# Moving tail products, a projection piece and an input scaling between the segments of a recurrent forward stage

## The chip, the core and the metric

The kernel runs on one core of one Trainium2 chip. A core has five engines with queues of their own: TensorE (PE in the profile; its weight loads are PEld), VectorE (DVE), ScalarE (ACT), GpSimd (POOL) and SyncE (SP, which here only issues DMAs). The metric is the device time of one launch in microseconds; it was 2993.81, the median of three runs (2991.97 to 2997.16).

## The reference

The program computes a forward pass and all its gradients (`jax.vjp`). Only the forward part of the attention is touched by the change. Its core, cut from the reference, with 2048 rows of width 512, 32 heads of 128, segments of 32 rows and a memory of 8 rows:

```python
mem = mem0
for s in range(n_seg):                       # 64 segments, one after the other
    xs = x[:, s * seg_len:(s + 1) * seg_len, :]
    h = jnp.concatenate([mem, xs], axis=1)   # 8 + 32 rows
    q, k, v = (einsum('btd,dhe->bhte', h, W) for W in (Wq, Wk, Wv))
    scores = einsum('bhqe,bhke->bhqk', q, k) * scale
    p = softmax(where(mask, scores, -1e9))
    o = einsum('bhqk,bhke->bhqe', p, v)
    o = einsum('bhte,hed->btd', o, Wo)
    mem = o[:, :M, :]                        # the next segment's memory
    outs.append(o[:, M:, :])
```

Ahead of it stands the modulation: `mod = silu(c) @ w_mod`, six rows of 512, two of which scale and shift the layer norm of `x` (the input to the segments), and four of which are needed only behind the attention. The memory rows of a segment's output are the first rows of the next segment's input, so the 64 segments form a recurrence.

## The kernel before

The forward stage is `phase2`: one Python loop over the segments (`for s in range(NS)`), with `s4 = s % 4`, the segment's place in its tile of four (128 input rows). Every engine's instructions run in the order in which the loop writes them: `self.pin(i0)` at its end ties each instruction to the one before it on the same engine. Work that doesn't belong to a segment's own chain is written into chosen places of the loop.

A segment's own chain, in its order on TensorE: projection of K and Q (`proj`, L673 and L257 by helper, 32 products each, in four column groups of 32), V chunk 0, the turn of K and Q (`turns`, L851), V chunk 1, the scores (`st_exp`, L861, exponentials on ScalarE at L863), V chunk 2, the row sums (`den`, L867) and the products with V (`pv`, L887), the scaling by the row sums into `Ost` (`ost`: L911 on VectorE, L908 on ScalarE), its transposes into `OT` (`ott_first`, `ott_rest`, L879 and L921), the out-projection (`outproj`, 64 products, L223), the split of its result into a rounded half `at_hi` (ScalarE, L230) and the rest `at_lo` (VectorE, L232), the fold that sums the four row groups (`sum_pair`, `at_ft`, L242), and the copy of the eight memory rows into the next segment's `hT` (L1065). That copy is where this document draws the border between segments.

A segment of 40 rows is 8 memory rows and 32 input rows, and the four column groups of TensorE hold 32 rows each. So 8 rows of each segment, its tail, are left over, and the tails of the four segments of a tile are done together:

- The tail rows of K and Q of tile t + 1 (`b_pieces`, from the input rows in `hb`, into RBk and RBq) are projected in tile t: K in two pieces of four steps, Q in pieces of two, four and two. The dictionary that `b_pieces` gives says in which segment and at which place a piece runs: `"turn"` is ahead of `ott_first`, `"f1"` is between the out-projection and the fold, `"f2"` is behind the copy into `hT`. `fill(s4, where)` runs what is entered in `slots`.
- The tail rows of V ride in the free fourth column group of the V chunks (`VTAILS`).
- The tail rows of the attention output are collected in `ao_tail` through a tile (`tail.collect`, POOL). Their 32 out-projection products come in pieces of 8, 16 and 8 (`TailRows`, `tail.chunk()`), into one PSUM tile `ao_tps`. When the third is done, `tail.split()` rounds it into `ao_b_hi` (ScalarE) and `ao_b_lo` (VectorE) and puts the fold on the list `later`; `pop_later` takes it from there in a following segment (`ao_b_ft`, eight small products), and one segment behind that come its transpose and four stores.

Also in the loop: the input tile's norm in five steps, `p1(j, k)`: k = 0 loads, 1 takes the statistics (VectorE, then a power on POOL), 2 scales (two VectorE instructions, L411 and L412), 3 shifts (L416, and a store), 4 turns the tile (four transposes on TensorE, then copies into `hx` and `hb`). Tile j is three tiles ahead in steps 0 to 2 and two in steps 3 and 4. And the sixteen pieces of the late modulation rows (`mod_rest`): one segment issues the load of 128 columns of `w_mod` on SP, the next one runs eight products at place f2, then a copy on ScalarE and a store on POOL. `mod_at` lists the segments of the products.

PSUM: all of this shares one ring of five buffers (tag "p"), the scores have three of their own. ScalarE also writes the mask into the score buffers (`mask_copy`). The places, in the order of the loop from the scores on:

```python
st_exp(0..2); v_chunk(s, 2); v_tails(s + 1)
if s4 == 3: tail.chunk()                # place A: eight tail products
den, pv, ost ...; fill(s4, "turn"); ott_first(); ott_rest(); outproj()
p1 ...; tails_in("kq", s + 1)           # ahead of the split
parts = self.split_pair(sb2, at_ps, "at")
fill(s4, "f1")
if s4 == 3: tail.chunk()                # sixteen
ft = self.sum_pair(...); copy into hT; masks; fill(s4, "f2"); modulation
if s4 == 3: tail.chunk()                # eight
tail.split(); self.store_rows(...)
```

Of the kernel before, what the change touches and what calls it, by code (L numbers as in the profile page):

```python
# [40 lines left out]
class K:  # L41
# [403 lines left out]
    def phase2(self):  # L445
# [15 lines left out]
        with ExitStack() as ctx:  # L461
# [43 lines left out]
            def p1(j, k=None, defer=None):  # L505
                if j < NT:
                    if j not in p1s:
                        p1s[j] = p1_tile(j)
                    for i in (range(1, 5) if k is None else [k]):
                        r = p1s[j][i]()  # L510
                        if r is not None:
                            if defer is None:
                                hxs[j] = r()
                            else:
                                defer.append(lambda: hxs.update({j: r()}))
# [102 lines left out]
            def b_pieces(t):  # L618

                bt = btails[t] = {}  # L620
                RBt = RB

                def proj_b(x, a, n, eng):
                    hb = hxs[t][1]
                    self.col_pass(psp, Ws[x], 0, lambda c: hb[:, c, :, :].rearrange("p s q -> p (s q)"), RBt[x], eng, steps=(a, n))
                    if a + n == 8:
                        store = lambda: rows_out(RBt[x], DR[x], t * nseg_t, nseg_t)
                        if t == 0:
                            first_stores.append(store)
                        else:  # L630
                            store()

                def turn_b(x):
                    bt[x] = btp.tile([128, 8, 128], BF16, name="b_cols" + x)
                    tp = psp.tile([128, 8, 128], BF16, name="turn_ps", tag="p")
                    for i in range(8):
                        nc.tensor.transpose(tp[:, i, :], RBt[x][:, i * 128:(i + 1) * 128], self.ident[:, :])

                    def f():
                        for hf in range(2):  # L640
                            self.evac(("act", "dve")[hf], bt[x][:, 4 * hf:4 * hf + 4, :], tp[:, 4 * hf:4 * hf + 4, :])

                    evacs.append(f)

                P = lambda x, a, n, eng: (lambda: proj_b(x, a, n, eng))
                T_ = lambda x: (lambda: turn_b(x))
                if t == 0:
                    return {"k": [P("k", 0, 4, "dve"), P("k", 4, 4, "dve"), T_("k")], "q": [P("q", 0, 4, "dve"), P("q", 4, 4, "dve"), T_("q")]}
                return {(0, "f1"): [P("k", 0, 4, "dve")], (1, "f1"): [P("k", 4, 4, "dve")], (1, "f2"): [P("q", 0, 2, "act")],
                        (2, "turn"): [T_("k")], (2, "f1"): [P("q", 2, 4, "dve")], (2, "f2"): [P("q", 6, 2, "act")],  # L650
                        (3, "turn"): [T_("q")]}

# [126 lines left out]
            first_tile = first_tile_steps()  # L779
            norms = []  # L780
            mod_r = []
            mod_at = sorted([4 * i + 4 for i in range(4 * DC - 1)] + [7])
            def rows_b(rb, b):

                for i in range(4):
# [38 lines left out]
            for s in range(NS):  # L824
                s4 = s % nseg_t
                if s4 == 2:
                    p1(s // nseg_t + P1_AHEAD + 1, 0)
                if s4 == 0:
                    slots = b_pieces(s // nseg_t + 1) if s + nseg_t < NS else {}
                hT = get_ht(s)  # L830
                hT_next = get_ht(s + 1) if s + 1 < NS else None
                QT, KT, Vst = XT["q"], XT["k"], Vsts[s % 2]
# [81 lines left out]
                def ott_first():  # L914
                    ps, n = transposes_part(Ost, 0, m=120)
                    self.evac("dve", part3(OT, 0)[:, 0:n, 0:120], ps)
# [82 lines left out]
                    v_tails(s + 1)  # L999
                if s < NS - 1:  # L1000
                    nc.sync.dma_start(VTr[:], Vst[:, :], transpose=True)
                if s4 == 3:
                    tail.chunk()
                or2 = ps_f32("or_ps")
                den(0, or2)
                den(1, or2)
# [8 lines left out]
                ost(0, or0, "dve")  # L1015
                ost(1, or1, "act")
                den(2, or2)
                early = s4 == 0 and len(self.later) > 1
                pv(2, or2)
                recip(2, 3, or2)  # L1020
                ost(2, or2, "dve")
                fill(s4, "turn")
                if s == 3 or s4 == 1 and s > 1:
                    p1(s // nseg_t + P1_AHEAD, 4, evacs)
                if s == NS - 1:
                    turn_v(2)
                ott_first()
                if early:
                    self.pop_later()
# [8 lines left out]
                nc.sync.dma_start(self.OSR[s], gl3(Ost))  # L1038
                at_ps = outproj()
                evac_turned()  # L1040
                if s < 3:
                    p1(P1_AHEAD, s + 1)
                if s4 != 1 and s > 0:
                    p1(s // nseg_t + P1_AHEAD + (s4 > 0), {2: 1, 3: 2, 0: 3}[s4])
                if NS - 4 <= s < NS - 1:
                    first_tile[s - NS + 4]()
                elif s == NS - 1:
# [1 line left out]
                if s + 1 < NS:  # L1049
                    tails_in("kq", s + 1)  # L1050
                parts = self.split_pair(sb2, at_ps, "at")
                tail.collect(s4, [OT])
                nc.sync.dma_start(self.OT[s], gl3(OT))
                fill(s4, "f1")
                if s == NS - 1:
                    first_tile[7]()
                    nc.scalar.activation(self.first_st[:, 11:12], self.first_st[:, 10:11], AF.Sigmoid)
                if s4 == 3:
                    tail.chunk()
                if s == NS - 1:  # L1060
                    turn_p(0)
# [9 lines left out]
                if s + 1 in mod_at:  # L1071
                    load, products = self.mod_rest(psp, sb2, mod_at.index(s + 1))
                    load()
                    mod_r.append(products)
                if s4 == 3:
                    tail.chunk()
                tail.split()
                self.store_rows(psp, sb2, ft, self.AOA[s + 1, 0:32, :], "at", "p")
# [1372 lines left out]
```

## Time and profile before

| | |
|---|---|
| median of three runs | 2993.81 us |
| the profiled execution | 2993.29 us, span 2991.5 us |
| forward loop | to about 970 us |
| segments 0, 1, 2, 3 of most tiles | 13.96, 13.96, 14.39, 15.23 us |
| TensorE's granted clock over the span | 0.996 |

The span runs from the first to the last instruction; 1.8 us of the profiled execution's time lie around it. In group lines the columns are line, engine, operation, written and read tiles, shapes and count. In the table of stretches each row is a stretch, its length, the busy time (and count) of PE, PEld, DVE, ACT and POOL, the granted clock, DMA share and GB/s. In the timeline each row is a start, a length, the engine and its instruction, and in brackets the idle time before it and what ended it. A product's length in the timeline contains some 0.2 to 0.4 us of passage through the array, so work on TensorE is read from start to start. A number "into" a segment counts from the copy into `hT` that starts it.

### The profile page before, as it was taken

The page shows a single profiled execution, that of the slowest core. Times are in us where ns is not written, and L with a number is a line of the kernel's source. Part 1 is how long each engine was busy: PE and PEld are TensorE (multiplying, and loading weights), DVE is VectorE, ACT ScalarE, POOL GpSimd, SP SyncE. Part 2 cuts the span into 40 slices and gives each one's busy share as a digit, 9 for nine tenths or more (in the row PEclk, how much of TensorE's full clock was granted, in tenths as well). Part 3 has the DMA queues.
Part 4 walks back from the last instruction along what each step waited for, and adds up shares of the span by engine and source line. Part 5 has one row for each costly group of instructions (what it writes and reads, how often), then busy time and mean ns, then how long its engine had stood idle before and what let it go on. Part 6 is the DMA issues. An engine that isn't in the chain of part 4 may idle for free.

```text
span 2991.5 us, 105396 instructions
## 1 busy us (share of the span) xinstructions
PE 2916.3 (97%) x43816; PEld 1819.9 (61%) x43816; DVE 1625.0 (54%) x3680; ACT 1347.8 (45%) x3244; POOL 1237.0 (41%) x2485
## 2 busy tenths in 40 slices
PE   6999999999999999999999999999999999999999
PEld 3666666666666544446577777777777754445455
DVE  5566556566555788833455566666556632850011
ACT  3666666666666533312355555555555520110011
POOL 2455555545555222221244444444444422762111
PEclk8999999999999999999999999999999999999999
DMA  9988888888889899998699999999999997786565
GB/s 308 223 224 212 213 211 221 212 216 213 213 214 274 211 231 232 230 277 285 202 248 243 250 251 240 258 256 252 249 252 254 245 280 247 251 263 193 158 217 172
DMA packets 837922, 703.01 MB, mean 235 GB/s; under 512 B 537682, under 2 KB 709890, under 8 KB 836548
## 3 DMA queue, kind: packets, MB, share of 16 engines
q1 hardware_dynamic: 711828, 485.29, 66.5%
q0 software_dynamic: 54512, 148.63, 15.8%
q10 hardware_dynamic: 71104, 62.34, 6.5%
q8 instruction: 345, 5.65, 0.8%
q14 instruction: 133, 1.09, 0.1%
HBM read 294.99 MB, written 276.35 MB: 191 GB/s over the span
## 4 chain that ended last, share of the span: by engine, by line
PE 65%; DMA 2%; DVE 1%; ACT 1%; issue 1%; POOL 0%; DVEq 0%; SPq 0%; POOLq 0%; ACTq 0%
PE gps L2232 14%; PE dh_ps L215 8%; PE g_ps L1855 5%; PE pass_ps L257 5%; PE gps5o L2247 4%; PE dhq_ps L223 4%; PE mm L1336 3%; PE dh_tps L215 3%; PE gps L1515 3%; PE mm L1296 2%; PE mm L1311 2%; PE tps L1772 2%; PE mm L1269 1%; PE mm L1265 1%; PE gps L1414 1%; PE dp_ps L1832 1%
## 5 line engine op out<-in xcount | busy, mean ns | idle before, releaser
L2232 PE MATMUL gps<-rows,hrows 128*128 128x512 bf16 (+2 forms) x2160 | 415.5, 356 | 0.0
L2232 PEld LDWEIGHTS <-hrows 128*128 128x128 bf16 x2160 | 211.2, 98 | 204.5 <-issue 0.9
L63 DVE CAST ot<-gps 128x512 bf16<-128x512 f32 (+3 forms) x76 | 48.2, 634 | 309.0 <-PE gps L2232 229.0
L1083 POOL TENSOR_TENSOR Pst<-Pst,rden 120x1408 bf16<-120x1408 bf16 x63 | 159.8, 2536 | 96.0 <-issue 54.3
L1900 POOL COPY dOst<-RAd 96x512 bf16<-96x512 bf16 x128 | 75.2, 611 | 300.5 <-DVE RAd L63 299.6
L61 ACT ACTIVATE ot<-gps 128x512 bf16<-128x512 f32 (+3 forms) x75 | 41.2, 549 | 350.5 <-PE gps L2232 215.1
L673 PE MATMUL pass_ps<-Wv,hT 128*32 128x512 bf16 (+2 forms) x2304 | 186.7, 357 | 0.0
L2236 POOL DMA_DIRECT2D out_dram<-ot x104 | 78.5, 755 | 256.0 <-DVE ot L63 132.9
L257 PEld LDWEIGHTS <-hT 128*32 128x32 bf16 x4096 | 115.3, 97 | 98.0 <-POOL hT L559 4.7
L63 DVE CAST Vst<-pass_ps 96x512 bf16<-96x512 f32 x128 | 87.1, 681 | 106.7 <-ACT RBv L61 98.1
L215 PE MATMUL dh_ps<-WvT,dVT 128*32 128x512 bf16 x2048 | 133.9, 381 | 1.8 <-DVE RBd L63 0.2
L223 PE MATMUL at_ps<-Wo,OT 128*32 128x256 bf16 x4096 | 128.8, 276 | 1.8 <-ACT OT L61 1.0
L673 PE MATMUL pass_ps<-Wv,hb 128*32 128x512 bf16 (+2 forms) x636 | 127.5, 349 | 2.2 <-DMA Wv<-in_A_Wv_dram 2.2
L257 PE MATMUL pass_ps<-Wk,hT 128*32 128x512 bf16 x2048 | 123.5, 382 | 2.5 <-DVE mv L402 1.1
L257 PE MATMUL pass_ps<-WoT,dyT 128*32 128x256 bf16 (+1 forms) x3072 | 123.3, 308 | 1.5 <-ACT dyT L1981 0.9
L223 PE MATMUL dhq_ps<-WqT,dQT 128*32 128x256 bf16 x4096 | 123.1, 273 | 0.4 <-issue 0.4
L257 PE MATMUL pass_ps<-Wq,hT 128*32 128x512 bf16 x2048 | 122.8, 379 | 0.0
L215 PE MATMUL dh_ps<-WkT,dKT 128*32 128x512 bf16 x2048 | 122.3, 380 | 0.0
L814 POOL DMA_DIRECT2D Vst<-RBv x192 | 100.9, 529 | 49.1 <-ACT ET L863 33.3
L2247 PE MATMUL gps5o<-WoT,rows 128*128 128x512 bf16 x560 | 121.0, 379 | 0.0
L223 PEld LDWEIGHTS <-dQT 128*32 128x32 bf16 x4096 | 110.0, 97 | 16.1 <-issue 0.6
L317 DVE TENSOR_TENSOR dST<-dh_ps,dST 128x512 bf16<-128x512 f32 x64 | 44.3, 692 | 130.3 <-ACT dST L316 130.3
(475 smaller groups left out, 7061.6 us busy)
## 6 DMA issues: line engine op xcount, KB each, us to landing
OSR<-Ost SPq DMA_DIRECT2D x64, 352.0 KB
OT<-OT SPq DMA_DIRECT2D x64, 352.0 KB
PS<-Pst SPq DMA_DIRECT2D x64, 352.0 KB
Pst_l<-PS SPq DMA_DIRECT2D x64, 352.0 KB
OT_l<-OT SPq DMA_DIRECT2D x64, 352.0 KB
DVR<-rows_x POOLq DMA_DIRECT2D x64, 352.0 KB, 6.5
DKR<-rows_x POOLq DMA_DIRECT2D x64, 352.0 KB, 5.8
DQR<-rows_x POOLq DMA_DIRECT2D x64, 352.0 KB, 3.3
```

Source lines behind the costliest of these rows:

```text
L63: return nc.vector.tensor_copy(out, in_)
L215: self.nc.tensor.matmul(ps[32 * j:32 * j + 32, :], lhsT=lhsT, rhs=w, start=(n < 4), stop=(n >= total - 4), tile_position=(0, 32 * j))
L223: nc.tensor.matmul(ps[32 * j:32 * j + 32, :], lhsT=x[k], rhs=w[k][:, 256 * d:256 * d + 256], start=(n == 0), stop=(n == total - 1), tile_p ...
L257: self.nc.tensor.matmul(ps[32 * j:32 * j + 32, :], lhsT=lhs(c), rhs=rhs, start=(c == 0), stop=(c == DC - 1), tile_position=(0, 32 * j))
L673: nc.tensor.matmul(ps[32 * j:32 * j + 32, o * E:(o + n) * E], lhsT=lhsT, rhs=wc[:, 3 * a + hl:3 * (a + n - 1) + hl + 1:3, :], start=(c == ...
L814: nc.gpsimd.dma_start(Vst[96 + 8 * j:104 + 8 * j, :], rb[32 * j + o:32 * j + o + 8, :])
L1083: nc.gpsimd.tensor_tensor(Pst[0:120, :, :], Pst[0:120, :, :], rden[:, :].unsqueeze(2).to_broadcast([120, G, 128]), op=ALU.mult)
L1336: nc.tensor.matmul(hp[:], lhsT=xT[:, fc, :], rhs=wT[:, fc, :], start=(n == 0), stop=(n == 2 * FC - 1))
L1515: nc.tensor.matmul(ps[:], lhsT=h2r[:, j, c * 128:(c + 1) * 128], rhs=xr[:, j, :], start=(j == 0), stop=(j == NT - 1))
L1855: nc.tensor.matmul(ps[:, j, 0:w], lhsT=lh[:, g * GW:(g + 1) * GW], rhs=rh[:, g * GW:g * GW + w], start=True, stop=True)
L2232: nc.tensor.matmul(ps[:, 0:ng * E], lhsT=hrows[:, tp_, c * 128:(c + 1) * 128], rhs=rows[:, tp_, 0:ng * E], start=(tp_ == 0), stop=(tp_ == ...
L2247: nc.tensor.matmul(pss[gg][:], lhsT=rows[:, t, gg * E:(gg + 1) * E], rhs=dyrows[:, t, :], start=(n == 0), stop=(n == NTP - 1))
```

## The change

Four moves, all in `phase2`:

- The three `tail.chunk()` calls go from segment 3 to segment 0 (`s4 == 0`) of the next tile, and the first of them from place A, ahead of the row sums, to just ahead of `ott_first`. The split of the tail, its fold, its transpose and stores follow one segment later than before (`early` now tests segment 1).
- The first K piece of the tail pass, which ran at f1 of segment 0 for the next tile, runs at f1 of segment 3, for the tile after the next (`b_pieces` now returns it apart).
- The modulation products go from segment 0 to segment 3 (`mod_at`), their loads from segment 3 to segment 2.
- The scaling of the input tile (`p1(..., 2)`) in segment 3 goes from ahead of `split_pair` to behind it. The first tile's steps are set one segment earlier, since its `hb` is now needed in segment 3: segment 0 does steps 1 and 2 of input tile 2, segment 1 step 3, segment 2 step 4.

```diff
-                return {(0, "f1"): [P("k", 0, 4, "dve")], (1, "f1"): [P("k", 4, 4, "dve")], (1, "f2"): [P("q", 0, 2, "act")],
+                return {(3, "f1"): [P("k", 0, 4, "dve")]}, {(1, "f1"): [P("k", 4, 4, "dve")], (1, "f2"): [P("q", 0, 2, "act")],
...
-            mod_at = sorted([4 * i + 4 for i in range(4 * DC - 1)] + [7])
+            mod_at = sorted([4 * i + 3 for i in range(4 * DC - 1)] + [4])
...
+                if s == 0:
+                    first_piece, pieces = b_pieces(1)
+                    slots[0, "f1"] = first_piece[3, "f1"]
                 if s4 == 0:
-                    slots = b_pieces(s // nseg_t + 1) if s + nseg_t < NS else {}
+                    slots.update(pieces)
+                if s4 == 3:
+                    first_piece, pieces = b_pieces(s // nseg_t + 2) if s // nseg_t + 2 < NT else ({}, {})
+                    slots.update(first_piece)
...
-                if s4 == 3:
-                    tail.chunk()
                 or2 = ps_f32("or_ps")
...
-                early = s4 == 0 and len(self.later) > 1
+                early = s4 == 1 and len(self.later) > 1
...
-                if s == 3 or s4 == 1 and s > 1:
+                if s == 2 or s4 == 1 and s > 1:
                     p1(s // nseg_t + P1_AHEAD, 4, evacs)
...
+                if s4 == 0:
+                    tail.chunk()
                 ott_first()
...
-                if s < 3:
-                    p1(P1_AHEAD, s + 1)
-                if s4 != 1 and s > 0:
-                    p1(s // nseg_t + P1_AHEAD + (s4 > 0), {2: 1, 3: 2, 0: 3}[s4])
+                for k in {0: (1, 2), 1: (3,)}.get(s, ()):
+                    p1(P1_AHEAD, k)
+                if s4 in (0, 2) and s > 0:
+                    p1(s // nseg_t + P1_AHEAD + (s4 > 0), {2: 1, 0: 3}[s4])
...
                 parts = self.split_pair(sb2, at_ps, "at")
+                if s4 == 3:
+                    p1(s // nseg_t + P1_AHEAD + 1, 2)
...
-                if s4 == 3:
+                if s4 == 0:
                     tail.chunk()
...
-                if s4 == 3:
+                if s4 == 0:
                     tail.chunk()
                 tail.split()
```

## The prediction

> **What bounds the kernel now.** I read the page first, for the engine that sets the end, then the busy times cut at the segments' borders, then the waits of TensorE between 67 and 948 us, and last the engines' timelines of one tile (segments 44 to 47) and the segment behind it. Busy shares and the chain that ended last come first.
>
> ```profile
> PE 2916.3 (97%) x43816; PEld 1819.9 (61%) x43816; DVE 1625.0 (54%) x3680; ACT 1347.8 (45%) x3244; POOL 1237.0 (41%) x2485
> ...
> PE 65%; DMA 2%; DVE 1%; ACT 1%; issue 1%; POOL 0%; DVEq 0%; SPq 0%; POOLq 0%; ACTq 0%
> ```
>
> TensorE carries the end. The change lies in the forward stage alone (its 64 segments end near 970 us), so only TensorE's waits and lengthened segments there matter. A border is the copy of the memory rows into `hT` (L1065); segment s runs from the copy that starts it to the next. Here are segments 1, 2, 3 of tile 11, segment 0 of tile 12, and segment 3 of tile 14 (length, then busy us of PE, PEld, DVE, ACT, POOL):
>
> ```profile
> 692.33:706.29 13.96, 13.79 (x274) 8.97 (x276) 7.84 (x20) 9.45 (x26) 4.93 (x7) 1.00 0.84 206
> 706.29:720.67 14.38, 14.06 (x285) 9.24 (x284) 8.99 (x23) 9.57 (x25) 9.77 (x21) 1.00 0.77 197
> 720.67:735.90 15.23, 14.56 (x301) 10.11 (x301) 9.01 (x22) 9.73 (x26) 8.81 (x21) 1.00 0.81 225
> 735.90:749.86 13.96, 13.58 (x275) 8.73 (x272) 8.53 (x21) 9.29 (x24) 6.70 (x14) 1.00 0.89 231
> ...
> 891.86:906.47 14.61, 14.45 (x301) 10.09 (x300) 7.95 (x20) 9.74 (x27) 6.45 (x13) 1.00 0.84 223
> ```
>
> See: 13.96 is a floor, held even by segments 60 to 62, whose waits have almost nothing to fill them: the chain of one segment's steps sets it, not TensorE's work. Segment 3 stands 1.27 above it, or 0.65 in tiles 13 and 14, where no input tile is left to scale. TensorE's waits in that stage (total us, times, longest):
>
> ```profile
> PE at_ft L242 <- DVE at_lo L232: 12.0, 26, 1.3
> PE tps L879 <- DVE Ost L911: 9.5, 32, 0.6
> PE tps L921 <- ACT Ost L908: 2.2, 14, 0.2
> ```
>
> The first is VectorE doing other work ahead of `at_lo`; the second is an unfilled hole before the attention output is transposed. Segment 47 (a segment 3), VectorE, then TensorE:
>
> ```profile
> 733.93 0.54 DVE L411 TENSOR_SCALAR xh<-x,mv,rstd 128x512 f32<-128x512 bf16 x1
> 734.50 0.71 DVE L412 TENSOR_TENSOR xh<-xh,ca_bc 128x512 f32<-128x512 f32 x1
> 735.13 0.41 DVE L232 TENSOR_TENSOR at_lo<-at_ps,at_hi 128x256 bf16<-128x256 f32 x1
> ```
>
> ```profile
> 728.94 0.60 PE L215 MATMUL ao_tps<-Wo,ao_tail 128*32 128x512 bf16 x5
> 729.47 0.35 PE L867 MATMUL or_ps<-ones,ET 128*128 128x1 bf16 x8
> ...
> 730.43 0.61 PE L637 MATMUL turn_ps<-ident,RBq 128*128 128x128 bf16 x8
> 730.97 0.38 PE L879 MATMUL tps<-ident,Ost 120*128 120x120 bf16 x4
> 731.52 0.53 PE L921 MATMUL tps<-ident,Ost 120*128 120x120 bf16 x7 [0.16 <-ACT Ost L908]
> ...
> 735.60 0.27 PE L242 MATMUL at_ft<-foldsel,at_lo 128*128 128x32 bf16 x4 [0.51 <-DVE at_lo L232]
> 735.79 0.61 PE L215 MATMUL ao_tps<-Wo,ao_tail 128*32 128x512 bf16 x8
> ```
>
> Segment 48 (a segment 0) has nothing between its products and its transposes:
>
> ```profile
> 744.90 0.33 PE L887 MATMUL or_ps<-Vst,ET 128*128 128x128 bf16 x3
> 745.62 0.39 PE L879 MATMUL tps<-ident,Ost 120*128 120x120 bf16 x4 [0.38 <-DVE Ost L911]
> ```
>
> **The change, part by part.** The sum goes against the profiled execution: span 2991.5, its own time 2993.29, which is 0.5 below the median of the three runs, 2993.81.
>
> *Scaling behind the split.* In segments 3 of tiles 1 to 12, L411 and L412 (0.54 and 0.71) leave the place ahead of `at_lo`. Segment 59, without them, shows the value: 15.23 - 14.61 = 0.62. Twelve times: -7.4. Segment 23 lost 0.74 more because both ran long there (0.92 and 1.07); that goes too: -0.7. Next late are the first tail evacuation of K (0.69), `at_tb` (0.45) and the next segment's first K cast, queued behind the two. From `at_lo`'s end, 13.77 in a segment of 14.13, this cast starts at 13.77 + 1.25 + 0.69 + 0.45 = 16.16, so 2.03 into segment 0. Today it starts there at 738.45, 2.55 in, behind the tail's `ao_b_lo`, in a 13.96 segment. Cost 0; bounds 0 and the 0.62.
>
> *First eight tail products out of segment 3's middle.* They stand between the last V chunk and the row sums (L867). Segment 3 of tile 0 has no tail products: its row sums come 8.36 behind its start (94.81 - 86.45), against 8.20 in segment 48 (744.10 - 735.90) and 8.80 in segment 47. The 0.17 stays (segment 3 evacuates two tail pieces of V where others do one), so segment 3 becomes 13.96 + 0.17 = 14.13, and tiles 1 to 14 gain 14.61 - 14.13 = 0.48 each: -6.7. Bounds: 0.44 (the difference of row-sum starts) and 0.65.
>
> *The same eight into segment 0.* Eight such products take 0.46 (from 735.79 to the next pass at 736.25). Segment 47's eight transposes at the same place take 0.54 (730.43 to 730.97) and segment 46's take 0.55 without a wait behind them. So they fit: 0. Bounds: 0, and the 0.48 that they cost in segment 3.
>
> *Swaps of equal work.* Segment 3's sixteen tail products (1.04) go to segment 0 and sixteen of K's tail pass (1.04) come back; eight modulation products (0.62) change places with eight tail products (0.61). Each covers the same `at_hi`/`at_lo` or `hT` wait: 0. Where both stand in one segment, that costs 0.42 (segment 8 is 14.38); this moves from segment 7's end to segment 4's: 0. The tail's `ao_b_hi` and `ao_b_lo` (0.59, 0.69) move to segment 1's start, which has the rest of today's segment 0: 0. RBk is read by its turn in segment 2 and is free.
>
> *The tail's fold into segment 1, its rows into segment 2.* Segment 1 already holds one PSUM tile for the input's turn; with `ao_b_ft` the second group of transposes must wait for a buffer, as in segment 47, where it began 0.55 behind the first group instead of 0.22, and the out-projection came 1.06 behind instead of 1.00. I take 0.06, fifteen times: +0.9; bounds 0 and 0.2 (the buffer freed by VectorE's last scaling, 0.13 later). Segment 2 gets the second transpose, which segment 1 has now at 13.96: 0. Its POOL queue gets four stores of 0.57 ahead of `rstd`, whose reader runs a segment later: 0.
>
> *Queues.* SP issues the modulation weights (0.48) in segment 2, behind the Q tail rows, so the stores and the transposing DMAs of segment 3 go 0.5 later. Covered by SP's idle 1.7 before the store of PS at 740.39 and 1.4 before 744.96.
>
> *Start and end.* In segment 0 the scaling of tile 2 comes ahead of `at_lo`, but VectorE idles 4.49 there: 0. Segment 2 loses the shift (0.68) that held `at_lo` (wait 0.92 against 0.31 in segment 46) and gets four transposes (+0.13): -0.5. Segment 3: 14.79 to 14.13, -0.6. The last segment loses 32 products (1.9 of TensorE) and a fold, but sixteen of them cover a wait: I take half, -1.0; bounds 0 and -1.9.
>
> Sum: -7.4 - 0.7 - 6.7 + 0.9 - 0.5 - 0.6 - 1.0 = -16.0, so 2993.3 - 16.0 = 2977.3.
>
> **The rivals.** *The hole in segment 0 does not take the eight products.* For it: the idle seen is 0.38, less than 0.46, and the engine changes from four narrow column groups to full transposes. Against: the 0.54 of turns fit. It gives 15 x 0.48 = 7.2 back: 2984.5.
>
> *The scaling is paid one segment later.* VectorE's two steps now meet POOL's `ao_tail` and `hT` copies (0.40 and 0.26). That they hinder each other is seen: Q's tail copies take 1.29 beside the scaling (segment 47) and 0.65 without it (segment 59), and in segment 23 VectorE was the loser. If the K cast slips behind the turn of K at 4.77, the 0.62 and segment 23's gain are lost: 2985.4. Segment 23 is why it keeps a chance. Against: even with its 0.74 the cast starts at 2.77 and Q's ends near 4.2. The Trainium skill, "SBUF — State Buffer", section "SBUF: two separate sides", calls VectorE's and GpSimd's shared port pair an exclusive lock on which the loser fully blocks. By that rule the scaling may stand still for a whole POOL copy; the rows agree that one of the two pays, and by 0.40 + 0.26 from them the cast would start at 2.69, and the sum stays.
>
> *Slower: the transposing DMA becomes the wait.* Place: segment 0's exponentials, 7.22 in, overwrite ET, which `Pst<-ET` of segment 3 must have read. In segment 1 they waited 1.85 for it. Today POOL's scaling of Pst starts at 1.93 and marks the landing; the change takes 1.10 (shorter segment 3) and 0.48 (the load) of the 5.3 left, so 3.7 remain. It decides from a further slip of 3.7 + 1.1 = 4.8; at 6 it costs 14 x 2.3 = 32: about 3009. Against: SP's idle above, and a DMA share of 0.81.
>
> *Nothing arrives*: another step of VectorE holds `at_lo`, and the hole does not take the products. Only the first tile and the end gain: about 2992. Segment 59's `at_lo`, which waits for `at_hi` alone, speaks against it.
>
> **How the numbers follow.** A measurement of this kernel tells about 0.2% (6 us) from no change. Chances: forecast 0.65, no hole 0.11, paid later 0.09, nothing 0.07, DMA 0.08. The likeliest gives 2977; its own bounds (0.2 in segment 1: +2; the end: +1 or -0.9; the 0.44 and 0.65: +0.6 or -2.4) give 2974 to 2981, and the next two rivals reach 2985.4, with 2 us of run-to-run spread 2987. I say 2973 to 2987. Faster 0.85, same 0.07, slower 0.08.
>
> **What would show it.** Segments 3 near 14.1, the others of a tile near 13.96, 14.0 and 14.4; `at_lo` waits of TensorE left in segments 2 alone; in segment 0 eight `ao_tps` products where 0.38 stood idle. Wrong if segment 0 grows towards 14.4, if its K turn comes later than 4.8, or if its exponentials wait for a DMA.

## The result, and the profile after

| | before | after |
|---|---|---|
| median | 2995.55 us (7 runs, 2991.97 to 3005.42) | 2984.12 us (7 runs, 2980.06 to 2987.78) |
| the profiled execution | 2993.29, span 2991.5 | 2986.66, span 2984.7 |

The ratio is 0.996, with an interval of 0.9946 to 0.9975: faster, by 7 to 16 us. The forecast was 2977.3. So the sign and the range held, but the point was 7 us too low, and an unaltered repeat of the changed kernel (first experiment) gave 0.9978 [0.9967, 0.9989]. Most of this part is about those lost microseconds: segments in which nothing waited came out as forecast, nearly to the hundredth, and something else gave part of the gain back.

The page of the changed kernel, busy times and the chain of work that ended last:

```profile
PE 2916.5 (98%) x43816; PEld 1817.4 (61%) x43816; DVE 1622.8 (54%) x3680; ACT 1348.8 (45%) x3244; POOL 1235.0 (41%) x2485
...
PE 69%; DMA 2%; ACT 1%; DVE 1%; issue 1%; SPq 0%; POOL 0%; DVEq 0%; ACTq 0%; POOLq 0%
```

TensorE still carries the end and does the same number of products. The table of stretches of the changed kernel, with the columns as before (length, busy us of PE, PEld, DVE, ACT, POOL, clock, DMA share, GB/s), gives first four segments in a row, 37 to 40 (places 1, 2, 3 and 0 of a tile), and then segments 45, 46, 48 and 62:

```profile
568.52:582.55 14.03, 13.87 (x281) 9.03 (x281) 8.00 (x20) 9.79 (x25) 6.61 (x15) 1.00 0.95 211
582.55:596.93 14.38, 14.05 (x286) 9.28 (x286) 9.13 (x24) 9.57 (x25) 7.44 (x12) 1.00 0.84 211
596.93:611.05 14.12, 14.11 (x291) 9.85 (x288) 8.29 (x21) 9.74 (x26) 8.18 (x21) 1.00 0.87 235
611.05:625.01 13.96, 13.96 (x277) 8.81 (x280) 8.92 (x21) 8.96 (x25) 7.46 (x15) 1.00 0.94 211
...
681.98:696.62 14.64, 14.06 (x281) 9.06 (x279) 8.00 (x20) 9.78 (x25) 8.62 (x22) 1.00 0.90 203
696.62:711.39 14.77, 14.24 (x286) 9.33 (x286) 9.14 (x24) 9.58 (x26) 7.46 (x12) 1.00 0.79 196
725.51:741.36 15.85, 14.17 (x277) 8.82 (x280) 8.91 (x21) 8.97 (x25) 7.25 (x15) 1.00 0.74 206
...
926.18:944.39 18.21, 13.88 (x234) 8.88 (x234) 7.93 (x19) 8.19 (x22) 8.19 (x16) 0.91 1.00 233
```

The first four are what was forecast: 14.03 (forecast 13.96 + 0.06), 14.38, 14.12 (forecast 14.13; 15.23 before) and 13.96 with eight more products in it. The last four are not: they have the same work in them as their like (45 as 37, 46 as 38, 48 as 40) and are 0.4 to 1.9 longer, and segment 62 is 4.3 longer than the 13.96 it took before. The waits of TensorE in the forward stage (67 to 944 us) say the same:

```profile
PE at_ft L242 <- DVE at_lo L232: 4.5, 15, 0.3
PE or_ps L873 <- ACT ET L869: 3.6, 10, 1.5
PE at_ps L223 <- DVE OT L63: 3.4, 2, 2.9
PE tps L885 <- DVE Ost L917: 3.2, 16, 0.4
```

The wait for `at_lo` fell from 12.0 to 4.5, fifteen times at most 0.3: thirteen stand in segments 2 (2 to 50), as said, and two of 0.2 in segments 59 and 61. That for `Ost` fell from 9.5 to 3.2, and from 32 times to 16. The wait for the exponentials (ET) is new, and that for `OT`, 0.4 before, grew to 3.4 by one wait near the end.

First what went right, in the timeline of segments 39 and 40 (border at 611.05), from the split of the one to the transposes of the next:

```profile
610.27 0.42 DVE L232 TENSOR_TENSOR at_lo<-at_ps,at_hi 128x256 bf16<-128x256 f32 x1 [0.49 <-ACT at_hi L230]
...
610.61 0.58 DVE L411 TENSOR_SCALAR xh<-x,mv,rstd 128x512 f32<-128x512 bf16 x1
...
611.23 0.69 DVE L412 TENSOR_TENSOR xh<-xh,ca_bc 128x512 f32<-128x512 f32 x1
...
620.31 0.61 PE L215 MATMUL ao_tps<-Wo,ao_tail 128*32 128x512 bf16 x8
620.86 0.38 PE L885 MATMUL tps<-ident,Ost 120*128 120x120 bf16 x4
```

`at_lo` waits for `at_hi` alone, the scaling comes behind it, and the eight tail products stand where TensorE was idle for 0.38, with no bracket behind the transposes that follow.

Now what went wrong. The timeline of segment 48 (border 725.51) of the changed kernel, with SyncE's issues (SPq) between the engines:

```profile
727.55 1.40 SPq L1007 DMA_TRANSPOSE VTr<-Vst  x1
729.05 1.50 SPq L1015 DMA_TRANSPOSE Pst<-ET  x1
...
734.61 1.40 ACT L869 ACTIVATE ET<-st_ps 128x480 bf16<-128x480 f32 x3 [2.36 <-DMA Pst<-ET]
734.64 2.54 POOL L1091 TENSOR_TENSOR Pst<-Pst,rden 120x1408 bf16<-120x1408 bf16 x1 [6.72 <-issue]
737.20 0.32 SPq L1094 DMA_DIRECT2D PS<-Pst  x1
...
740.57 2.83 SPq L1007 DMA_TRANSPOSE VTr<-Vst  x1
```

Segment 47's exponentials are transposed out of ET by the DMA of 729.05, issued 3.54 *behind* the border. In the kernel before, the same DMA, of its segment 47, was issued at 733.67, which is 2.23 *ahead* of the border at 735.90. The exponentials of segment 48, which overwrite ET, wait 2.36 for it (they could start 7.22 in, and start 9.10 in). The norm on GpSimd, which scales what the DMA wrote, starts with them; its result is stored by SyncE at 737.20, and only behind that store come, in SyncE's queue, the K and Q stores and the next transposing DMA, again late. Segments 44, 45, 46, 48, 49 and 52 are longer by this, 5.3 us together.

Segment 62 is the same lateness in another place:

```profile
932.17 0.42 SPq L740 DMA_DIRECT2D b_colsk<-MODROW  x1
932.71 0.37 SPq L1061 DMA_DIRECT2D OT<-OT  x1
939.05 0.93 ACT L61 ACTIVATE OT<-tps 128x480 bf16<-128x480 bf16 x2 [2.66 <-DMA OT<-OT]
...
939.88 3.25 PE L223 MATMUL at_ps<-Wo,OT 128*32 128x256 bf16 x64 [2.87 <-DVE OT L63]
```

The store of segment 61's `OT` is issued behind four loads of modulation rows, 6.5 into segment 62, and the copies that overwrite `OT` wait 2.66 for it. TensorE waits 2.87, and then its clock drops: the stretches 938 to 944.39 of this kernel have granted clocks of 0.81, 0.50 and 0.87, and the 64 products take 2.98 from first start to last instead of 1.69 (segment 40).

```profile
938.00:940.00 2.00, 0.12 (x4) 0.12 (x8) 0.58 (x3) 0.93 (x2) 0.00 (x0) 0.81 1.03 389
940.00:942.00 2.00, 2.00 (x43) 1.49 (x43) 1.29 (x3) 0.00 (x0) 1.75 (x4) 0.50 1.58 189
942.00:944.39 2.39, 1.67 (x36) 1.03 (x28) 0.42 (x1) 0.38 (x1) 2.39 (x9) 0.87 0.63 105
```

So border 41 (end of segment 41) lies 9.71 us earlier than before, and border 62 only 3.94. The prediction had named exponentials that wait for a DMA as a sign of being wrong; in segments 45, 48, 49 and 52 the trace has that sign.

### The profile page after: what moved, and what is told of

Its sections match the earlier page's. It is cut to its first block, busy times and chain, and to the rows that moved or that the text cites. A ratio compares the mean times of both kernels' runs of the same rounds, so it can differ in the third digit from the quotient of the medians.

```text
span 2984.7 us, 105439 instructions
## 1 busy us (share of the span) xinstructions
PE 2916.5 (98%) x43816; PEld 1817.4 (61%) x43816; DVE 1622.8 (54%) x3680; ACT 1348.8 (45%) x3244; POOL 1235.0 (41%) x2485
## 3 DMA queue, kind: packets, MB, share of 16 engines
q0 software_dynamic: 54512, 148.63, 15.7%
## 4 chain that ended last, share of the span: by engine, by line
PE 69%; DMA 2%; ACT 1%; DVE 1%; issue 1%; SPq 0%; POOL 0%; DVEq 0%; ACTq 0%; POOLq 0%
PE gps L2240 14%; PE dh_ps L215 8%; PE pass_ps L257 7%; PE g_ps L1863 5%; PE gps5o L2255 4%; PE dhq_ps L223 4%; PE mm L1344 3%; PE dh_tps L215 3%; PE gps L1523 3%; PE mm L1304 2%; PE mm L1319 2%; PE tps L1780 2%; PE mm L1277 1%; PE mm L1273 1%; PE gps L1422 1%; PE dp_ps L1840 1%
## 5 line engine op out<-in xcount | busy, mean ns | idle before, releaser
L223 PEld LDWEIGHTS <-OT 128*32 128x32 bf16 x4096 | 99.3, 98 | 25.7 <-ACT OT L61 6.4
```

Source lines behind the costliest of these rows:

```text
L223: nc.tensor.matmul(ps[32 * j:32 * j + 32, :], lhsT=x[k], rhs=w[k][:, 256 * d:256 * d + 256], start=(n == 0), stop=(n == total - 1), tile_p ...
```

## The experiments

Two theories first. CHANCE: the late DMA belonged to this one execution. QUEUE: with shorter tiles SyncE has too little time for its DMAs, the lateness of one segment is handed to the next, and it always comes to such waits. All kernels of a group ran on one chip with runs of the kernel before among them; its median was 2991.42 in the first group, 2994.64 in the second and 2991.63 in the third, so ratios are compared across groups, not times.

### The change again, unaltered

> The changed kernel once more, unaltered. Two theories. CHANCE: the late transposing DMAs of its first profile (exponentials waiting for Pst<-ET by 1.1 to 2.4 us in segments 44 to 52, OT waiting in segment 62) belonged to that execution. Then this profile has such a wait in segment 1 alone, border 62 stands 12 to 14 us earlier than before's 948.33, and the time is 13 to 16 us under before. QUEUE: a tile that is 1 us shorter leaves SyncE too little time for its issues; the transposing DMA of every segment is issued 1 to 5 us into the next one instead of 1.7 us ahead of its border, and here and there it lands behind 7.22 us, where the exponentials overwrite ET. Then the waits come back, in the same stretch of tiles or another, 3 to 10 us in all, and the time is 9 to 12 us under before. Both: segments 3 at 14.12, segments 1 at 14.03, segments 2 at 14.39.

Measured: 2985.72, ratio 0.9978 [0.9967, 0.9989]. The waits came back, in part in other places: segments 24 (15.70, a wait of 2.22), 44 (14.74) and 45 (14.63) for the transposing DMA, segments 2 and 26 for the load of an input tile from the same queue (`x`, 1.07 and 1.31; segment 27, 15.81, behind it lost its time ahead of the exponentials), and segment 62 (17.59) for the store of `OT`.

```profile
384.39:400.09 15.70, 14.16 (x277) 8.85 (x279) 8.90 (x21) 8.96 (x24) 7.44 (x15) 1.00 0.91 215
414.27:430.06 15.79, 14.07 (x286) 9.30 (x286) 9.22 (x24) 9.57 (x25) 7.58 (x13) 1.00 0.83 204
671.93:686.67 14.74, 14.17 (x277) 8.83 (x280) 8.91 (x21) 8.96 (x24) 5.42 (x7) 1.00 0.88 215
...
926.92:944.51 17.59, 14.21 (x234) 8.92 (x234) 7.93 (x19) 8.19 (x23) 8.51 (x17) 0.90 0.99 254
```

CHANCE falls in so far as both profiled executions have such waits. Only one execution of each kernel is profiled, and this one took 2992.99, near the top of its runs (2978.54 to 2993.78), so how much of the waits the quicker executions have isn't known.

### The change, with the scaling ahead of the split again

```diff
                 if s4 in (0, 2) and s > 0:
                     p1(s // nseg_t + P1_AHEAD + (s4 > 0), {2: 1, 0: 3}[s4])
+                if s4 == 3:
+                    p1(s // nseg_t + P1_AHEAD + 1, 2)
...
                 parts = self.split_pair(sb2, at_ps, "at")
-                if s4 == 3:
-                    p1(s // nseg_t + P1_AHEAD + 1, 2)
```

> The changed kernel with the scaling of the input tile back ahead of the split in segment 3. Both theories: segments 3 of tiles 1 to 12 go from 14.12 to about 14.74 (0.62 for at_lo's wait). CHANCE: 12 x 0.62 and no waits for DMAs, so 7 to 8 us slower than the changed kernel. QUEUE: the tile is longer by 0.62, SyncE catches up by as much in each, the waits of segments 44 to 52 disappear, and only 2 to 5 us are lost.

Measured: 2987.21, 0.9981 [0.9973, 0.999]. Segment 3 is 14.74, so the scaling is worth 0.62 a tile as forecast. But the kernel lost only 1.5 us against the repeat, not 7.4: from segment 6 to 62 no exponentials start more than 0.3 late (1.9 in segment 48 above), and segment 62 was 14.51. The two kernels can't be told apart by their intervals. Where a tile is 0.62 longer, the lateness goes away, and with it nearly as much time as the longer tiles cost.

### The scaling alone, in the kernel before

```diff
-                if s4 != 1 and s > 0:
-                    p1(s // nseg_t + P1_AHEAD + (s4 > 0), {2: 1, 3: 2, 0: 3}[s4])
+                if s4 in (0, 2) and s > 0:
+                    p1(s // nseg_t + P1_AHEAD + (s4 > 0), {2: 1, 0: 3}[s4])
...
                 parts = self.split_pair(sb2, at_ps, "at")
+                if s4 == 3:
+                    p1(s // nseg_t + P1_AHEAD + 1, 2)
```

> The kernel before with one part of the change alone: the scaling in segment 3 behind the split. Both theories: segments 3 of tiles 1 to 12 go from 15.23 to 14.61, and segment 23's stretch to 15.97 does not recur, so 7.4 to 8.2 us under before. QUEUE adds: the issue of the transposing DMA in segments 3 and 0 comes some 0.6 us later against the border, with no wait of the exponentials behind segment 1.

Measured: 2981.33, 0.9963 [0.9952, 0.9975]. Segment 3 is 14.61, the others 13.96, 13.96 and 14.39. This one line of the change gives as much as the whole of it. So either the moved tail products gain nothing, or what they gain is taken away again.

### The eight tail products in segment 0, but ahead of the row sums

```diff
+                if s4 == 0:
+                    tail.chunk()
                 or2 = ps_f32("or_ps")
...
-                if s4 == 0:
-                    tail.chunk()
                 ott_first()
```

> The changed kernel with the first eight tail products in segment 0 ahead of the row sums instead of ahead of the output's transposes (the old place, in the new segment). If the hole before the transposes is what hides them, segment 0 grows from 13.96 to 14.4 and the hole of 0.38 comes back; 15 x 0.46 = 7 us slower by CHANCE, 2 to 5 by QUEUE, which gives the longer tile its lost waits back. If they are hidden anywhere (a rival of the forecast's reading), segment 0 stays at 13.96.

Measured: 2986.53, 0.9983 [0.9974, 0.9992]. Segment 48 of this kernel, which is 15.85 in the changed kernel's profile and 13.96 in the kernel before:

```profile
728.62:742.99 14.37, 13.98 (x277) 8.90 (x279) 8.87 (x21) 8.95 (x24) 7.25 (x15) 1.00 0.97 210
```

Segment 0 is 0.41 longer, so ahead of the transposes the eight products do cost nothing: the hole takes them. Yet this kernel is level with the repeat (2985.72), and from segment 6 to 62 its exponentials start at most 0.3 late. Three times now a longer tile was paid for by waits that vanished.

### Lateness, segment by segment

The traces of these five kernels can be put on one scale: the end of SyncE's issue of `Pst<-ET` of a segment, less the border behind that segment. Negative is ahead of the border. The columns are means, by the segment that starts at the border. The last two columns are the mean length of the tiles from segment 13 to 52, and then the segments in which exponentials were held up (the first three segments are left out).

```
kernel                 seg 10-23  24-39  40-52  53-61   tile
before                   -1.29   -0.73  -0.93  -0.98   57.64  nothing
scaling alone             2.66    0.12  -0.65  -1.14   56.95  segment 4 (a wait of 0.75)
tail ahead of sums       -0.16   -0.10  -0.44  -0.83   56.95  at most 0.3 in segments 6 to 62
scaling ahead             2.35    0.95  -0.49  -0.68   57.16  at most 0.3 in segments 6 to 62
the change                0.95    2.37   3.89   2.06   57.04  44 to 46, 48, 49, 52
the change, repeat        3.31    3.17   3.96   2.39   57.21  23, 24, 44, 45
```

Where tiles take 56.95 or more by their own work, lateness drains. In the changed kernel a tile is 14.03 + 14.38 + 14.12 + 13.96 = 56.49 of work, and lateness grows until the waits make the tile longer.

Why does it feed itself? In SyncE's queue the order of a segment is: VTr, Pst (the two transposing DMAs), stores of OSR and OT, in two of four segments six pieces of K or Q tail rows, store of VT, store of PS, then the K and Q stores and the next VTr and Pst. The store of PS waits for the norm on GpSimd (2.54), which waits for Pst to land. So the next Pst stands, through the queue, behind the landing of the last one: from the issue at 729.05 above to the next at 743.49, 14.44 us, with 5.59 to the norm's start, 2.54 of norm, and then the issues from PS to VTr. Theory LOOP: it is this circle, of about 14 us, that the short segments meet. Rival LOAD: the DMA engines are full.

SyncE's idle time shows how tight the queue is. It has two places for it. Ahead of VTr it waits for the segment's own V (at 744.96 of the kernel before, for ScalarE's last piece of Vst, done at 744.93), which is real slack; ahead of PS it waits for the norm, which is part of the circle. Read from its timelines, in segments 12 to 51 the first, beyond the 0.23 that always stand there, was 1.70 us a tile before and is 0.08 in the change and 0.10 in its repeat. The second went from 6.6 to 7.1. So SyncE waits for the segments' own work no more. It waits for the norm in segments 0 and 1 of a tile; in segments 2 and 3, which have the six pieces, it issues without a pause, so there its own issue time fills the segment (44.4 us of a tile's 56.9 are issues).

### The store of PS from GpSimd's queue

```diff
                     nc.sync.dma_start(self.VT[s], VTr[:])
-                    nc.sync.dma_start(self.PS[s], Pst[:])
+                    nc.gpsimd.dma_start(self.PS[s], Pst[:])
```

> The whole change, with one edit: the store of the softmax weights (PS<-Pst) is issued from GpSimd's queue, right behind the multiplication that it waits for, and no longer from SyncE's. Two theories for the gain that was given back. LOOP: the lateness feeds itself through SyncE's queue: transposing DMA of the exponentials -> marks and landing -> norm on GpSimd (2.53) -> PS store, and behind that store in the queue the K and Q stores (2.6 to 4.0), the transposing DMA of V (1.3 to 2.3) and the next one of the exponentials; round this loop a segment takes about 14, as long as the shortened segments are. LOAD: the DMA engines (busy share 0.85 to 0.91 in these segments, before and after alike) are simply full, whatever the order. Expected by LOOP: the K and Q stores go out without waiting for the norm, the transposing DMAs are issued 2 us or more earlier, no wait of the exponentials for them, segment 62 about 14.5 and not 17.6 to 18.2: 2985 - 5.3 - 3.5, some 2976 (2973 to 2980). Expected by LOAD: the waits stay, 2984 to 2987; above that if GpSimd's own queue now holds something up.

Measured: 2984.36, 0.9959 [0.9947, 0.9971]. The profile (an execution of 2978.56) shows what LOOP said: lateness -0.64, -0.74, -0.76 and -1.10 on the scale above, one exponential that waits (1.9, in segment 1), tiles of 56.54, segment 62 at 13.95, and border 62 15.7 us earlier than before. SyncE's idle time ahead of VTr is back, at 6.8 us a tile. The median shows it only in part: the six runs go from 2977.58 to 2987.70, and only one is profiled. As a time this is a miss by 8 us, and the interval doesn't tell it from the change's own (0.9946 to 0.9975).

The same edit in the kernel before:

> The control for the first of these runs: the kernel before, with the same store (PS<-Pst) issued from GpSimd's queue. In the kernel before, lateness drains by segment 10 and no exponentials wait, so both theories expect little: 0 to -2 us against before. If it gains as much as the edit gains in the changed kernel (8 or more), the edit is worth something by itself and the theory of a loop that only the shorter segments meet falls. By LOOP the difference between the two edited kernels is the forecast's full sum, about -13 to -16.

Measured: 2997.81, 1.0007 [0.9997, 1.0017]. By itself the edit is worth nothing, or costs a few us (expected: 0 to -2). Changed against unchanged kernel, both with the edit, is 2984.36 - 2997.81 = -13.4.

### The exponentials' transposing DMA ahead of V's

```diff
+                Pst = sb2.tile([128, G, 128], BF16, name="Pst", bufs=1)
+                if s < NS - 1:
+                    nc.sync.dma_start(Pst[:], ET[:, :], transpose=True)
                 if s < NS - 1:
                     nc.sync.dma_start(VTr[:], Vst[:, :], transpose=True)
...
-                Pst = sb2.tile([128, G, 128], BF16, name="Pst", bufs=1)
-                if s < NS - 1:
-                    nc.sync.dma_start(Pst[:], ET[:, :], transpose=True)
-                else:
+                if s == NS - 1:
                     nc.gpsimd.dma_start(self.w_up, ...)
```

> The whole change, with the transposing DMA of the exponentials (Pst<-ET) put ahead of that of V (VTr<-Vst) in SyncE's queue; both theories as for the run before. The same DMAs and bytes; only the exponentials' one goes out 1.3 to 2.3 us earlier, and V's later by as much. LOOP: two of the loop's 14 us lie outside it now, so that lateness drains: no wait of the exponentials (5.3 us back, in the profile and about as much elsewhere), part of segment 62's loss back too: 2976 to 2981. LOAD: only the bound that lateness hits is moved off by 2 us; lateness still grows, waits come later and are as long: 2983 to 2987.

Measured: 2979.17, 0.9947 [0.9935, 0.9959], the profiled execution 2976.49. And again, in the third group:

> The whole change with the exponentials' transposing DMA ahead of V's, unaltered from the earlier run of it, now beside the three others on one chip. LOOP (lateness fed through SyncE's queue, which the swap shortens): about 15 under before, ratio 0.9945 to 0.9955, no steady wait of the exponentials. If the earlier run was a lucky one: 9 to 11 under before, as the change without the swap.

Measured: 2977.04, 0.9955 [0.9942, 0.9969]. The repeat's segments 45 to 48 and 62, which were 14.64, 14.77, 14.12, 15.85 and 18.21 in the changed kernel's profile:

```profile
680.19:694.21 14.02, 13.86 (x281) 9.02 (x280) 8.00 (x20) 9.78 (x26) 8.59 (x22) 1.00 0.85 203
694.21:708.59 14.38, 14.06 (x286) 9.27 (x285) 9.13 (x24) 9.57 (x25) 7.43 (x12) 1.00 0.83 223
708.59:722.71 14.12, 14.11 (x291) 9.84 (x288) 8.29 (x21) 9.73 (x26) 8.15 (x21) 1.00 0.77 222
722.71:736.68 13.97, 13.97 (x277) 8.78 (x280) 8.92 (x21) 8.96 (x25) 7.25 (x15) 1.00 1.06 228
919.21:933.16 13.95, 12.50 (x234) 8.06 (x234) 7.94 (x19) 8.19 (x22) 6.66 (x10) 1.00 0.97 255
```

And its order of DMAs around the border at 694.21:

```profile
689.34 1.79 SPq L1008 DMA_TRANSPOSE Pst<-ET  x1
691.39 1.39 SPq L1010 DMA_TRANSPOSE VTr<-Vst  x1
...
695.31 2.54 POOL L1091 TENSOR_TENSOR Pst<-Pst,rden 120x1408 bf16<-120x1408 bf16 x1 [0.74 <-DMA Pst<-ET]
```

The DMA of the exponentials is out 3 us ahead of the border, the norm starts 1.10 behind it (7.67 in the same segment of the changed kernel), and lateness stays at -3.19, -3.16, -2.90 and -3.48. That is 4 to 7 us less late than in the change, where the swap itself moves this DMA by the length of one issue (1.9 in the median). Not a byte is moved less. The load says the same: the share of the 16 DMA engines that the hardware queue took in the forward stage, first before, then after:

```profile
q1 hardware_dynamic: 257990, 179.57, 81.9%
```

```profile
q1 hardware_dynamic: 257570, 179.46, 81.6%
```

It is the same in the kernel without the waits and in the kernel with them, and in the two profiles with the swap, which have no such waits behind segment 1, it is 82.4 and 82.2% (to 933 us). LOAD falls; the cause was what stood behind what in one queue.

The same swap in the kernel before:

> The kernel before with the same swap of the two transposing DMAs: the control. LOOP: lateness drains there without it, so the swap is worth 0 to -2 (a little in the first eight segments at most). If the swap is worth 5 or more here too, it is a gain by itself and no part of the story of the change.

Measured: 2995.84, 1.0014 [1.0006, 1.0023]: slower, by 2 to 7 us. Neither theory said that. Its profile has border 62 2.25 us later than before. Segments 13 (14.32 for 13.96), 22 (14.76 for 14.39), 24 (14.24 for 13.96), 31 (15.53 for 15.23) and 49 (14.31 for 13.96) are longer, and in them the scaling into `Ost` starts 0.1 to 0.35 late; the same five are longer in the next kernel. What holds the scaling there isn't shown: the trace puts a wait down to the store OSR, which reads `Ost`, in segment 1 alone.

### The parts against each other, with the queue out of the way

The kernel before, with the swap and with the scaling behind the split (the two diffs above).

> The kernel before with the swap and with one part of the change, the scaling behind the split; the tail products and everything else stay where they were. It prices the parts against each other with lateness out of the way. By the terms of the prediction: the scaling gives 8.1, the tail products' move 6.7 less 0.9 for the fold; so 8 under the kernel before with the swap, and 6 to 7 over the whole change with the swap. If the tail products' move is worth nothing whatever the queue does (as the scaling alone, which came out as fast as the whole change, would have it), it is level with the whole change with the swap, within 2.

Measured: 2987.35, 0.9986 [0.9977, 0.9995]. That is 8.5 under the kernel before with the swap (forecast for the scaling: 8.1), and 10.3 over the whole change with the swap (forecast for the rest: 6 to 7). So the tail products' move does gain, once lateness doesn't take it. The 10.3 is more than the segments explain: in the profiles segments 4 to 59 take 798.65 and 790.82, a difference of 7.8. Of it 6.9 is segment 3 (14.61 against 14.12, fourteen times), and 1.4 are the longer segments 13, 22, 31 and 49, which this kernel shares with the one above; the fold in segment 1 takes 0.5 back.

### Both edits together

The swap and the store of PS from GpSimd's queue, in the changed kernel.

> The whole change with both edits: the swap, and the store of the softmax weights from GpSimd's queue. LOOP: either edit alone already drains the lateness, so the two together give no more than one: level with the swap alone, within 2. LOAD (the DMA engines are the bound and each edit only moved it off): each would add, 3 to 6 under the swap alone.

Measured: 2977.57, 0.9956 [0.9944, 0.9969]: level with the swap alone. That agrees with LOOP: what one edit frees, the other can't free again.

### Two other stores from GpSimd's queue

```diff
-                nc.sync.dma_start(self.OSR[s], gl3(Ost))
+                nc.gpsimd.dma_start(self.OSR[s], gl3(Ost))
...
-                nc.sync.dma_start(self.OT[s], gl3(OT))
+                nc.gpsimd.dma_start(self.OT[s], gl3(OT))
```

> The whole change, with two other stores taken out of SyncE's queue: OSR<-Ost and OT<-OT are issued from GpSimd's. The bytes stay, SyncE has 1.1 to 2.5 us a segment less to issue. LOOP: in the segments in which SyncE issues without a pause (those with six pieces of K or Q, at 0.58 to 0.63 each) that time comes straight off its lateness; in the others it goes into the wait for the norm; so the waits of the exponentials vanish, and segment 62's last store no longer stands behind four other loads: 2975 to 2981. LOAD: 2984 to 2987. Under either, GpSimd's queue would now wait for the attention output (OSR) before its other work; if the copies that it makes come late by that, slower than 2987.

Measured: 3090.22, 1.0329 [1.0315, 1.0342]: 96 us slower, where a gain of 4 to 10 was expected. In its forward stage the exponentials wait for the transposing DMA nearly everywhere:

```profile
L1015 SPq DMA_TRANSPOSE Pst<-ET x57: 1712/2943/4298, 60.9 to 938.6; - x57
...
  DMA Pst<-ET: 84.2, 43
```

The issue of that DMA takes 2.94 in the median, against 1.83 in the changed kernel, and the waits of the exponentials up to 945 us alone are 84.2 us. The expectation had feared GpSimd's own queue, but GpSimd waits under 4 us in all for these two stores (200 to 940 us). Why the transposing DMAs become slower when the two stores of 352 KB go through the other queue stays open. By LOOP this edit should have gained, so LOOP doesn't tell all that sets the length of a DMA's issue.

## Why the prediction was right, and where it was off

Against the steps of the prediction, with segments 4 to 59 summed by their place in the tile. "With the swap" is the repeat of that kernel, whose queue is out of the way; the change's own sum for the 56 segments is 795.89, against 805.23 before and 790.82 with the swap.

| step | forecast | measured |
|---|---|---|
| scaling behind the split (with segment 23) | -8.1 | segments 3 with the scaling alone: 212.73 to 204.78, -7.9 |
| eight tail products out of segment 3 | -6.7 | 204.78 to 197.70 with the swap, -7.1; segment 3 forecast 14.13, measured 14.12 |
| the same into segment 0 | 0 | 196.15 to 195.85, -0.3; 0.4 each where the hole isn't used |
| swaps, segment 2 | 0 | 200.80 to 200.59, -0.2 |
| the fold in segment 1 | +0.9 | 195.54 to 196.67, +1.1, of which 0.4 is segment 5, where the modulation products now stand beside the tail's (segment 8, a segment 0, is 0.4 shorter for it) |
| start, segments 2 and 3 | -0.5, -0.6 | 14.99 to 14.45, 14.79 to 14.12: -0.5, -0.7 |
| end | -1.0 | from border 62 to the next stage's first product 22.19 to 21.56: -0.6 (21.56 and 26.73 in the two with the swap) |
| queues | 0 | +5.1 in segments 4 to 59 (795.89 - 790.82), +4.3 in segment 62 |

- **The terms of TensorE and VectorE were right**, each within 0.4 us over the whole stage. K's first cast in segment 0 starts 1.62 in (forecast 2.03), its turn 4.77 (the bound was 4.8). With the swap the span is 17.2 and 16.8 under before, the forecast's sum 16.0; at border 62, ahead of what the change doesn't touch, it is 15.2 and 15.0, against 15.0 forecast without the end.
- **The step that failed is "Queues"**, "Covered by SP's idle 1.7 before the store of PS at 740.39 and 1.4 before 744.96". The 1.7 were not spare. SyncE stood there waiting for the norm, which waited for a transposing DMA that SyncE itself had issued; when everything in the circle comes later, that wait moves along and covers nothing. The 1.4 were a wait for the segment's own V, and so true slack, but there was only 1.70 us of it a tile, and the shorter tile used it up (0.08 left). In place of 0 the term measured about 9 us in the profiled execution.
- **The slower rival had the right wait and the wrong arithmetic.** It named the exponentials that overwrite ET, in segments 0 (three of the six longer segments are such), and counted 1.10 + 0.48 against a slack of 5.3, once. The lateness is handed from tile to tile: issue ends drift from 0.95 behind the border (segments 10 to 23) to 3.89 (40 to 52), so a fixed slack is used up after enough tiles. It also had the price wrong, 2.3 in each of 14 tiles: each wait makes the loop wait too, so the waits take back only what the tiles were too short. That is why it cost about half of the gain and did not end slower. The prediction didn't foresee that limit. That the time still fell inside its range was in part luck: the term's 9 us just fit below the upper end, which lay 9.7 above the point.
- **"The hole does not take the products" falls** by the table above and the run with the products ahead of the row sums. **"The scaling is paid one segment later" falls**: segments 0 take 13.96 to 14.07 from segment 4 to 40. (Its remark that one of the two engines pays is too simple for segment 23 before: VectorE's pair took 1.99 for 1.25, and of GpSimd's two copies beside it one took 0.85 for 0.64.) **"Nothing arrives" falls.**
- **The start** was more scattered than a term of 0.5. Segment 1 took 15.19 before, 18.55 in the changed kernel's profile (its exponentials wait 2.94 for the transposing DMA), and 13.83 and 16.89 in the two with the swap; the granted clock averages 0.90 from 45 to 80 us in the changed kernel, 0.85 in the first of the two with the swap and 0.85 before. How much of that is the queue and how much the clock isn't separated.
- The best kernel of these runs is the change with the swap: 2979.17 and 2977.04, in ratios 0.9947 and 0.9955 to the kernel before.

## What to carry to other kernels

An issuing queue is an engine with a chain of its own: before idle time in it is used as cover, look at what ends that idle time, and if it is work that the queue itself feeds, it is no cover. Where a loop is shortened, ask of every queue whether it still drains within one turn; if it doesn't, the slack between it and its reader is not a margin but a countdown, and a late wait far from the change is the sign. And when two parts of a change add up to less than one of them alone, look for what both push against, and free that before either is judged.

## What the runs showed of the hardware

- The issue of a transposing DMA holds SyncE's queue for 1.28 to 3.64 us (median 1.86 in the forward stage of the change), where the stores of K and Q from RA0 and RA1 take 0.49 in the median but up to 2.3. Which of two of them goes first was worth some 2 to 9 us in the changed kernel (ratios of 0.996 and 0.9978 against 0.9947 and 0.9955), at the same bytes. The Trainium skill, "DMA: Bandwidth & Descriptors", section "Issuing engines are not separate DMA queues", says that issuing on several engines only saves time on the sequencer, which is usually small. Here it wasn't small, with issues filling 44.4 of the 56.9 us of a tile, and the order on it cost time at an unchanged share of the DMA engines (81.6 to 82.4%).
- The same edit, sending stores through GpSimd's queue, was harmless for one store (PS) and cost 96 us for two others (OSR and OT).
- A wait of 2.87 us of TensorE in segment 62 cost 4.3: the granted clock fell to 0.50 behind it, and the 64 products took 2.98 for 1.69. TensorE's longest wait in segments 44 to 52, 1.5 us, left the clock at 1.00. The Trainium skill, "TensorE: Matmul & The Clock Gate", section "Part 1: The HAM clock gate", puts the fall behind an idle window of about 3.4 us that runs freely. The trace agrees in the half rate; the idle time here, 2.87, was shorter than that.
